# Sliding-window attention in quarter-array matmuls, with K, V and Q in natural order

## Chip, cores, metric

The kernel runs on one core of one Trainium2 chip. The metric is the device time of one launch in microseconds (us), lower is better. A run counts as slow when it is over 1.5% above the fastest of the same kernel; the ratios below use the other, fast runs alone.

## The reference

Eight samples, eight heads, 576 tokens, head size 64. Attention looks 32 tokens to each side; its result is the input of a two-layer MLP with 4608 tokens, 512 features and 2048 hidden units.

```python
scores = scale * np.matmul(q, k.transpose(0, 1, 3, 2))
mask = np.abs(pos[:, None] - pos[None, :]) <= 32
scores = np.where(mask, scores, -1e9)
attn = softmax(scores)                      # cut: written out with max, exp, sum
attn_out = np.matmul(attn, v)
x = attn_out.transpose(0, 2, 1, 3).reshape(B * S, H * D)
r = np.maximum(x @ w_in, 0.0)
out = (s * (r * r) + b) @ w_out             # float32 in and out
```

The kernel computes in bf16. The MLP is most of the work: for one sample of 576 tokens it takes 144 matmuls of 512 columns. At the 216 ns that one takes in the traces this is 31.1 us per sample.

## The kernel before: the parts that matter

The program first builds a list of tasks. Each has an engine (`pe`, `act`, `dve`, `pool`, `sp`), a list of instructions, an assumed cost in ns, what it reads and what it writes. A planner orders the tasks of every engine with those costs and sets the waits. On the chip each engine then runs its own list strictly in that order. Nearly all DMAs are issued by one engine, SP, so SP's list is a queue: an issue that is slow, or that waits, holds up every later one.

The samples from the third on (`b >= 2`) are prepared while the MLP of earlier samples runs. This is what SP does for 256 tokens of q or of k; rows of two tokens keep the pieces at 512 bytes, and one issue transposes all 256 tokens:

```python
def chunk(b, t0, n, key):                       # n = 128, 128, 32: 256, 256 and 64 tokens
    for name in "qk":
        add("sp", lambda e: e.dma_start(        # one load, 512-byte pieces
            STG[si][0:n, 0:1024].rearrange("p (h c) -> p h c", h=H),
            src_of[name][b, :, t0:t0 + 2 * n, :].rearrange("h (p i) d -> p h (i d)", i=2)),
            570.0, ...)
        add("dve", lambda e: e.tensor_copy(NAT[ni]..., STG[si]...), 680.0, ...)
        add("sp", lambda e: e.dma_start(        # one transposition of 128 x 1024
            dst[:, :, :, t0 // 2:t0 // 2 + n].rearrange("p i a s -> p (i a) s"),
            NAT[ni][0:n, :, :].rearrange("p i c -> p (i c)"), transpose=True),
            2500.0 * n / 128, ...)              # <- the assumed cost goes by size
    ...                                         # cut: DVE copies k into block diagonals KBD
```

v comes in 16 loads per sample issued by POOL. Attention on PE takes two heads at a time: K and V lie in block diagonals, so half of every 128 x 128 stationary matrix is zeros:

```python
fns = [lambda e: e.matmul(SC[:, par, pr * 128:pr * 128 + w],
       lhsT=KBD[:, pr, j, :], rhs=QT[slot][:, :, pr, lo // 2:hi // 2], ...) for pr in range(NPAIR)]
...                                             # cut: exp on ACT, mask on DVE
fns.append(lambda e: e.matmul(av[0:nr, pr, 0:130], lhsT=buf[:, pr, col:col + nr],
                              rhs=VBD[slot][:, j, pr, 0:130], ...))
...                                             # cut: XN = av / sum on DVE
add("sp", lambda e: e.dma_start(XT[:, :, ...], XN[xi][...], transpose=True), 1250.0, ...)   # b >= 3
```

The last line brings a result into the layout that the MLP reads. It too goes through SP's queue. For the first three samples (`XPE = 3`) PE does it. PE runs the visits of attention between the MLP's matmuls, as fillers of one list.

The softmax here doesn't subtract the row's maximum and nothing guards it: scores larger than these inputs give would overflow.

## Time and profile before

| | before |
|---|---|
| time, median of 3 runs | 330.35 us (329.95 to 333.12) |
| span of the profiled run | 329.0 us, mean granted clock 0.995 |
| PE busy | 307.3 us (93%) |
| MLP matmuls after 64 us, at their nominal spacing | 225.0 us |
| attention on PE after 64 us | 35.3 us |
| everything else on PE after 64 us (standing, slow clock) | 1.0 us |

The last three rows are worked out from the trace: each matmul is given the time from its start to the start of the next one, and an MLP matmul is charged 216 ns per 512 columns; what it takes beyond that is "everything else". In the kernels with quarters 93 ns per visit, the way into a visit (see below), are counted as attention. In the trace of before 31 of the 1344 records of MLP matmuls are missing, so its rows are good to about 1 us.

These lines are from the page of the kernel before. The row of 40 digits gives PE's busy tenths in 40 equal slices. The chain is the work that ended last, followed back from the end. In the group lines the columns are busy time, mean ns of one, and idle time of the engine before them with what ended it. In the lines of DMA issues they are KB each and us from issue to landing. The lines that begin with q are DMA queues: packets, MB, and the time that their packets took, as a share of the span of 16 DMA engines.

```profile
span 329.0 us, 5870 instructions
PE 307.3 (93%) x2212; PEld 179.6 (55%) x2245; DVE 207.8 (63%) x494; ACT 162.4 (49%) x275; POOL 87.4 (27%) x136
...
PE   1778989699999999999999999999999999999995
...
DMA packets 105372, 56.56 MB, mean 172 GB/s; under 512 B 54144, under 2 KB 97664, under 8 KB 105344
...
q1 hardware_dynamic: 100736, 49.10, 66.2%
q0 software_dynamic: 4608, 7.08, 10.5%
...
PE 71%; DMA 12%; SPq 8%; POOL 4%; issue 2%; DVE 1%; ACT 1%; ACTq 0%; DVEq 0%
...
L437 POOL DMA_DIRECT2D vst<-in_v_dram x96 | 59.0, 622 | 106.1 <-PE sc L548 60.5
...
L526 DVE COPY kbd<-kt 64x512 bf16<-64x512 bf16 (+1 forms) x72 | 18.6, 258 | 0.9
...
stg<-in_q_dram SPq DMA_DIRECT2D x16, 512.0 KB, 5.8
```

From the ninth slice on PE has nines alone, but for the last. The table of windows for 64 to 256 us says the same; its last line sums six stretches of 32 us:

```profile
sum 192.00, PE 190.32 PEld 106.67 DVE 142.47 ACT 100.15 POOL 54.45; mean PE 31.72 PEld 17.78 DVE 23.75 ACT 16.69 POOL 9.07
```

PE is the limit. The next lines are the views of SP's two lines in `chunk`, loads (L506) and transpositions (L519), with the time of one issue on SP as least/median/most in ns:

```profile
L506 SPq DMA_DIRECT2D stg<-in_q_dram x18: 333/396/2352, 55.3 to 224.8; - x18
L506 SPq DMA_DIRECT2D stg<-in_k_dram x18: 368/453/1953, 55.7 to 225.5; - x18
```

```profile
L519 SPq DMA_TRANSPOSE qt<-nat x18: 1174/1380/3882, 67.3 to 237.8; - x18
L519 SPq DMA_TRANSPOSE kt<-nat x18: 1192/1430/3731, 71.8 to 239.6; - x18
```

A transposition holds SP for 1.2 us at best and 1.4 us in the median. These medians mix two sizes. Told apart by the order of the issues, the 24 of 256 tokens, which the program books at 2500 ns, take 1.23 us at best and 2.07 us in the median (up to 3.88), and the 12 of 64 tokens, booked at 625 ns, take 1.17 and 1.26 us. So a quarter of the tokens is far from a quarter of the price.

### The profile page before, as it was taken

How to read it: one execution, taken by the hardware profiler on the slowest of the kernel's cores; microseconds unless marked ns; L12 is line 12 of the kernel's file. 1: busy time of each engine (PE TensorE's matmuls, PEld its weight loads, DVE VectorE, ACT ScalarE, POOL GpSimd, SP SyncE). 2: the span in 40 equal slices, each digit the busy share in tenths (PEclk: the TensorE clock that was granted, in tenths of full speed). 3: DMA queues.
4: the chain of work that ended last, by engine and by line, in shares of the span. 5: the costliest groups of instructions: out<-in, count | busy, mean ns of one | idle time of the engine just before them, and what ended most of it. 6: DMA issues, size and time to landing. Idle time of an engine off the chain costs nothing.

```text
span 329.0 us, 5870 instructions
## 1 busy us (share of the span) xinstructions
PE 307.3 (93%) x2212; PEld 179.6 (55%) x2245; DVE 207.8 (63%) x494; ACT 162.4 (49%) x275; POOL 87.4 (27%) x136
## 2 busy tenths in 40 slices
PE   1778989699999999999999999999999999999995
PEld 0567878576655565456545654555455544444442
DVE  6566577368867786869587857866876453323411
ACT  6686588146754672467236736541664433333300
POOL 8562341940560055014602440253000000000000
PEclk9999999799999999999999999999999999999999
DMA  8999999996599679968997998499913111000021
GB/s 212 227 368 356 299 179 266 290 203 156 136 238 212 159 160 216 194 179 229 203 253 125 230 224 194 133 201 244 225 36 75 51 46 62 34 32 34 32 85 76
DMA packets 105372, 56.56 MB, mean 172 GB/s; under 512 B 54144, under 2 KB 97664, under 8 KB 105344
## 3 DMA queue, kind: packets, MB, share of 16 engines
q1 hardware_dynamic: 100736, 49.10, 66.2%
q0 software_dynamic: 4608, 7.08, 10.5%
q8 instruction: 17, 0.28, 0.4%
q14 instruction: 11, 0.09, 0.1%
HBM read 36.70 MB, written 9.44 MB: 140 GB/s over the span
## 4 chain that ended last, share of the span: by engine, by line
PE 71%; DMA 12%; SPq 8%; POOL 4%; issue 2%; DVE 1%; ACT 1%; ACTq 0%; DVEq 0%
PE o L721 31%; PE w L702 30%; SPq L437 5%; DMA stg<-in_moe_w_out_dram 5%; PE avn L588 5%; DMA vst<-in_v_dram 4%; PE sc L548 3%; POOL vst L437 3%; DMA stg<-in_moe_w_in_dram 3%; SPq L461 2%; PE o L744 1%; POOL wout L420 1%; SPq L417 1%; DVE outs L734 0%; PE avn L610 0%
## 5 line engine op out<-in xcount | busy, mean ns | idle before, releaser
L702 PE MATMUL w<-xt,win 128*128 128x512 bf16 (+2 forms) x684 | 139.3, 340 | 1.3 <-ACT r L709 0.3
L721 PE MATMUL o<-wout,gt 128*128 128x512 bf16 (+1 forms) x629 | 139.8, 358 | 0.7 <-DVE outs L734 0.2
L709 ACT ACTIVATE r<-w 128x512 bf16<-128x512 f32 x144 | 85.9, 598 | 91.8 <-PE w L702 80.2
L711 DVE TENSOR_TENSOR gt<-r 128x512 bf16<-128x512 bf16 x144 | 60.9, 431 | 59.1 <-ACT r L709 58.1
L721 PEld LDWEIGHTS o<-wout,gt 128*128 128x128 bf16 x640 | 60.7, 98 | 57.6 <-DVE outs L734 0.7
L702 PEld LDWEIGHTS w<-xt,win 128*128 128x128 bf16 x704 | 62.0, 98 | 52.4 <-ACT r L709 0.8
L437 POOL DMA_DIRECT2D vst<-in_v_dram x96 | 59.0, 622 | 106.1 <-PE sc L548 60.5
L734 DVE SCALAR_TENSOR_TENSOR outs<-o,sb,cvec 128x512 f32<-128x512 f32 (+1 forms) x40 | 27.6, 692 | 19.1 <-PE o L721 17.5
L450 ACT CAST vbd<-vst 64x1024 bf16<-64x1024 f32 (+1 forms) x15 | 16.6, 1140 | 24.0 <-DMA vst<-in_v_dram 23.9
L565 ACT ACTIVATE exe<-sc 128x512 bf16<-128x512 f32 (+1 forms) x40 | 22.2, 554 | 10.8 <-PE sc L548 10.6
L588 PE MATMUL avn<-vbd,exo 128*128 128x130 bf16 (+1 forms) x224 | 26.1, 221 | 0.6 <-ACT xt L613 0.6
L548 PE MATMUL sc<-qt,kbd 128*128 128x128 bf16 (+1 forms) x288 | 25.2, 222 | 1.0 <-ACT exe L565 0.8
L548 PEld LDWEIGHTS sc<-qt,kbd 128*128 128x128 bf16 x288 | 20.2, 100 | 8.7 <-issue 1.0
L601 DVE TENSOR_TENSOR xn<-avn,rec 128x512 bf16<-128x512 f32 (+1 forms) x36 | 24.6, 683 | 0.3
L588 PE MATMUL avn<-vbd,exe 128*128 128x130 bf16 (+1 forms) x144 | 23.8, 221 | 0.5 <-ACT vbd L450 0.5
L511 DVE CAST nat<-stg 128x1024 bf16<-128x1024 f32 (+1 forms) x36 | 24.0, 682 | 0.1
L588 PEld LDWEIGHTS avn<-vbd,exo 128*128 128x128 bf16 (+1 forms) x224 | 20.8, 105 | 3.4 <-ACT xt L613 0.7
L565 ACT ACTIVATE exo<-sc 128x512 bf16<-128x512 f32 x32 | 19.2, 600 | 2.0 <-PE sc L548 2.0
L526 DVE COPY kbd<-kt 64x512 bf16<-64x512 bf16 (+1 forms) x72 | 18.6, 258 | 0.9
L588 PEld LDWEIGHTS avn<-vbd,exe 128*128 128x128 bf16 (+1 forms) x144 | 15.4, 110 | 3.2 <-ACT vbd L450 0.6
L598 DVE RECIPROCAL rec<-avn 128x8 f32<-128x8 f32 (+1 forms) x36 | 7.3, 204 | 13.7 <-PE avn L588 13.5
L571 DVE TENSOR_TENSOR exe<-exe,mask 128x512 bf16<-128x512 bf16 (+1 forms) x30 | 11.7, 389 | 4.8 <-ACT exe L565 4.7
(74 smaller groups left out, 152.1 us busy)
## 6 DMA issues: line engine op xcount, KB each, us to landing
stg<-in_q_dram SPq DMA_DIRECT2D x16, 512.0 KB, 5.8
stg<-in_k_dram SPq DMA_DIRECT2D x16, 512.0 KB, 7.4
out_dram<-outs SPq DMA_DIRECT2D x32, 256.0 KB, 2.3
vst<-in_v_dram POOLq DMA_DIRECT2D x96, 72.0 KB, 5.9
stg<-in_moe_w_in_dram SPq DMA_DIRECT2D x8, 512.0 KB, 8.5
stg<-in_moe_w_out_dram SPq DMA_DIRECT2D x8, 512.0 KB, 8.9
vst<-in_v_dram SPq DMA_DIRECT2D x16, 144.0 KB, 4.4
stg<-in_q_dram SPq DMA_DIRECT2D x8, 128.0 KB, 7.4
```

The lines of the kernel that those rows point to most:

```text
L437: add(stream, lambda e, dst=dst, src=src: e.dma_start(dst, src), 640.0 if stream == "sp" else 700.0, writes=[("VST", h, x) for x in (range ...
L511: add("dve", lambda e, si=si, ni=ni: e.tensor_copy(NAT[ni][0:n, :, :].rearrange("p i (h d) -> p h i d", h=H), STG[si][0:n, 0:1024].rearran ...
L526: add("dve", lambda e, i=i, p0=p0: e.tensor_copy(KBD[p0:p0 + 64, :, j0:j0 + nj, p0 + 32 * i:p0 + 32 * i + 32], KT[p0:p0 + 64, i, :, t0 // ...
L548: fns = [lambda e, j=j, pr=pr, lo=lo, hi=hi, w=w, par=par: e.matmul(SC[:, par, pr * 128:pr * 128 + w], lhsT=KBD[:, pr, j, :], rhs=QT[slot] ...
L565: add("act", lambda e, src=src, dst=dst: e.activation(dst.rearrange("p a (c i) -> p a c i", i=2), src, AF.Exp, bias=0.0, scale=0.125), 190 ...
L588: fns.append(lambda e, pr=pr, buf=buf, col=col, j=j, x=x, last=len(parts) - 1: e.matmul(av[0:nr, pr, 0:130], lhsT=buf[:, pr, col:col + nr] ...
L601: add("dve", lambda e: e.tensor_tensor(XN[xi][0:nr, :].rearrange("p (a b c) -> p a b c", a=4, b=2), av[0:nr, :, 0:128].rearrange("p a (b c ...
L702: add("pe", [lambda e, g=g, kc=kc: e.matmul(wt[:, g, :], lhsT=WIN_BF[:, kc, (f0 + g) * 128:(f0 + g + 1) * 128], rhs=XT[:, kc, t0 % XR:t0 % ...
L709: add("act", lambda e: e.activation(rt, wt, AF.Relu, bias=0.0, scale=1.0), 190 + 0.833 * 512, reads=[("W", wb)], writes=[("R1", rb)], key=key)
L711: add("dve", lambda e: e.tensor_tensor(GT[gs][:, f0:f0 + ng, g0:g0 + nt], rt, rt, ALU.mult), 130 + 0.53 * 512, reads=[("R1", rb)], writes= ...
L721: add("pe", [lambda e, fc=fc: e.matmul(O[:, ob, 0:cn], lhsT=GT[gs][:, fc, g0:g0 + 128], rhs=WOUT_BF[:, fc, c0:c0 + cn], start=(fc == 0), s ...
L734: add("dve", lambda e: e.scalar_tensor_tensor(OUTS[us][:, 0:cn], O[:, ob, 0:cn], SB128[:, 0:1], CVEC[:, c0:c0 + cn], ALU.mult, ALU.add), 2 ...
```

## The change

The intent: use TensorE as four independent quarters of 64 x 64. One head and 64 keys fit a quarter, so no block diagonals and no zeros are needed. Four scores, or four products with v, run at a time. The products with v of one unit (128 keys) and the scores of the next share one visit of PE. Without block diagonals, q, k and v can lie in natural token order, which saves the copies into the diagonals. The core of the diff:

```diff
-        KBD = sb((128, NPAIR, NTILE, 128), BF16, "kbd")
-        VBD = [sb((128, NTILE, NPAIR, VW), BF16, "vbd") for _ in range(2)]
+        KT = [sb((128, NPAIR, S), BF16, "kt") for _ in range(2)]
+        VB = [sb((128, NUNIT, H, VW), BF16, "vb") for _ in range(2)]
 ...
         def chunk(b, t0, n, key):
+            nx, np_ = (2, 128) if n == 256 else (1, n)
             for name in "qk":
-                add("sp", lambda e, si=si, name=name: e.dma_start(
-                    STG[si][0:n, 0:1024].rearrange("p (h c) -> p h c", h=H),
-                    src_of[name][b, :, t0:t0 + 2 * n, :].rearrange("h (p i) d -> p h (i d)", i=2)),
-                    570.0, ...)
+                add("sp", [lambda e, si=si, name=name, x=x: e.dma_start(
+                    STG[si][0:np_, x * 512:x * 512 + 512].rearrange("p (h d) -> p h d", h=H),
+                    src_of[name][b, :, t0 + 128 * x:t0 + 128 * x + np_, :].rearrange("h p d -> p h d"))
+                    for x in range(nx)],
+                    600.0 * nx, ...)
 ...
-                add("sp", lambda e, ni=ni, dst=dst: e.dma_start(
-                    dst[:, :, :, t0 // 2:t0 // 2 + n].rearrange("p i a s -> p (i a) s"),
-                    NAT[ni][0:n, :, :].rearrange("p i c -> p (i c)"), transpose=True),
-                    2500.0 * n / 128, ...)
+                add("sp", [lambda e, ni=ni, dst=dst, x=x: e.dma_start(
+                    dst[:, :, t0 + 128 * x:t0 + 128 * x + np_], NAT[ni][0:np_, x, :], transpose=True)
+                    for x in range(nx)],
+                    1250.0 * nx * np_ / 128, ...)
 ...
+        def load_v(b, t, key, waits=()):        # 5 loads a sample on SP, in place of 16 on POOL
+            add("sp", lambda e: e.dma_start(VST[0:n, t, :, :],
+                v[b, :, 128 * t:128 * t + n, :].rearrange("h p d -> p h d")), 640.0, ...)
 ...
+            fns = [lambda e, pr=pr, j=j, hp=hp: e.matmul(
+                SC[64 * (j % 2):64 * (j % 2) + 64, hp, pr * 128:pr * 128 + 128],
+                lhsT=KT[slot][64 * hp:64 * hp + 64, pr, 64 * j:64 * j + 64],
+                rhs=QT[slot][64 * hp:64 * hp + 64, pr, 64 * j:64 * j + 128], start=True, stop=True)
+                for pr in range(NPAIR) for j in tiles(u) for hp in hps]
 ...                                             # cut: products with v, joint visits, first two samples
-                cuts = [x0] + [x for x in range(XR, B * S, XR) if x0 < x < x0 + nr] + [x0 + nr]
+                cuts = {x0, x0 + r1 - r0} | {x for x in range(XR, B * S, XR) if x0 < x < x0 + r1 - r0}
+                cuts = sorted(cuts | ({x0 + WIN} if u == 0 else set()))   # one result transposition more a sample
```

The diff has three more parts: the loads of later samples may start earlier (`PACE`, the unit of the previous sample's attention that a load waits for, goes from 0 to 3 down to -1 to 1, where -1 is the last unit of the sample before that), NAT has 4 buffers in place of 6, and EX has 5 in place of 3.

## The prediction

> **What bounds the kernel now.** The span is 329.0 us (330.35 us by the clock). The chain that ended last is 71% PE; in the table of windows PE is busy 190.3 of 192.0 us between 64 and 256 us and 69.3 of 70.5 us after that. By matmul starts in the timeline, 64 to 326 us hold about 226 us of dense products (216 ns per 512-column matmul) and 34 us of attention, nothing idle. Before 64 us PE does only about 42 us of full-clock work (estimate: counts times 56 ns per 128 columns); there the chain is loads and casts of weights, the last w_out piece landing at 57.5 us; PE stands 2.8 us before the last column sum, then runs it at a reduced clock. DMA is 90 to 100% busy there, but moves 212 to 227 GB/s in the first 16 us (q, k, v) and 356 to 368 in the slices of weights.
>
> **Attention on PE, per sample from the third on:** 36 score matmuls at 56 ns (44 at the edges) and 52 value matmuls at 57: 4.86 us, 0.97 us a unit, 29 us for six samples.
>
> **What the change does.** Half of each of those matmuls multiplies zeros. Now 16 score matmuls (64x64, 128 columns) and up to 32 value matmuls (65 columns) per unit run four at a time: estimate 4 x 56 = 0.22 us and 8 x 29 = 0.24 us. The Trainium skill ("TensorEngine Tiling (Array Packing)", Key Properties) says that tiles work in parallel and that a change of tiling mode drains TensorE; no record of before shows such a change. A 128-column matmul lasts 220 ns at a spacing of 56: about 165 ns for a drain (estimate); one entering, one leaving and part of the wait between the value halves: about 0.33 us. Visit: 0.79 us instead of 0.97, 30 visits: minus 5.4 us, all on the saturated engine. The second sample saves about 1 us more.
>
> Against it: the first two samples' q and k are transposed in 144 blocks each in place of 48: about 2 us of PE more each; the first sample's visits are split, several us more, but PE idles there.
>
> **Moved off the other engines:** copies into block diagonals (18.6 us DVE), casts of v on ACT (16.6) and DVE (12), 96 loads issued by POOL (59 us). None was on PE's path after 64 us. Later q and k come in 256-byte pieces, v leaves the software queue: DMA roughly even, but SP issues about 20% more.
>
> **Start:** pairs of heads are loaded in 2304-byte pieces. At the weights' rate the 4.7 MB of q and k of two samples would take 13 us instead of 21. I count 3 to 5 us of earlier weights, shortening the hole at 57 to 64 us, less about 1.5 for the added PE work.
>
> **Sum:** 330.4 - 5.4 - 1 - 4 + 1.5, less about 2 for smoother supply = 319 us; range 312 to 326. Faster 0.75, same 0.23, slower 0.02.
>
> **To see:** a visit of about 0.8 us between dense matmuls; weights landed near 52 us; PE without idle after 60 us; dense products still at 216 ns.
>
> **What would make it wrong:** weight loads of 64 columns not running in parallel (a visit of 1.2 us or more, the gain gone); three full drains a visit; a longer first sample delaying the first dense matmul (23.8 us); SP issue or DMA falling behind from 60 to 240 us, so that PE starves.

## More of the kernel before

The timeline of SP shows how much room it has; its columns are start, us, what:

```profile
116.31 0.39 SPq L506 DMA_DIRECT2D stg<-in_q_dram  x1
117.36 1.28 SPq L618 DMA_TRANSPOSE xt<-xn  x1
120.25 0.40 SPq L506 DMA_DIRECT2D stg<-in_k_dram  x1
121.39 1.20 SPq L618 DMA_TRANSPOSE xt<-xn  x1
123.05 0.37 SPq L506 DMA_DIRECT2D stg<-in_q_dram  x1
124.19 2.48 SPq L618 DMA_TRANSPOSE xt<-xn  x2
```

There are gaps of 0.5 to 1.6 us between issues. Summed over 80 to 280 us, SP's issues take 125.5 of 200 us.

## The result

The changed kernel takes 369.52 us (median of 4 runs, 368.26 to 371.17); the kernel before, on the same chip, 330.56 us. The ratio is 1.1163, with a 95% interval of 1.1099 to 1.1227: slower. A ratio here and below is the mean time of one kernel's fast runs over that of the other's of the same rounds, so it is not quite the ratio of the medians.

| | before | after |
|---|---|---|
| span of the profiled run | 329.0 us | 369.4 us |
| mean granted clock | 0.995 | 0.949 |
| MLP matmuls after 64 us, at nominal spacing | 225.0 us | 226.9 us |
| attention on PE after 64 us | 35.3 us | 27.7 us |
| everything else on PE after 64 us | 1.0 us | 46.8 us |

So the attention saved 7.6 us of PE, as hoped, and PE lost 45.8 us by standing and by a slower clock. (The 12 gaps on PE of over 0.4 us after 64 us sum to 32 us; the rest, about 15 us, is mostly the slower clock.) With the 1.9 us of the first row the sum is 40.1 of the 40.4 us between the spans. Everything lies after 64 us. The profiled run is the slowest of the four and the one with the lowest clock; the others had 0.961 to 0.977.

The same lines of the page, after:

```profile
span 369.4 us, 8204 instructions
PE 319.2 (86%) x3452; PEld 169.3 (46%) x3452; DVE 176.7 (48%) x376; ACT 141.7 (38%) x217; POOL 42.6 (12%) x64
...
PE   3679997979699569674999997979699999999996
...
PEclk9999999899889889995999998998989999999999
...
DMA packets 150661, 56.71 MB, mean 154 GB/s; under 512 B 137312, under 2 KB 142432, under 8 KB 150624
...
q1 hardware_dynamic: 150624, 56.19, 66.1%
...
PE 54%; DMA 18%; SPq 17%; DVE 6%; issue 3%; ACT 1%; POOL 0%; DVEq 0%
...
stg<-in_q_dram SPq DMA_DIRECT2D x24, 256.0 KB, 4.2
```

PE's row has holes from the seventh slice to the 29th (about 55 to 268 us), roughly as long as SP prepares attention; then it is full again. All other engines became less busy, as intended. The share of SP's queue in the chain that ended last doubled from 8 to 17%. The DMA engines did not get more to do: the packets of the two queues before took 76.7% of 329.0 us, 252 us, and those of the one queue after 66.1% of 369.4 us, 244 us, although there are 43% more of them. The windows of 64 to 256 us, summed:

```profile
sum 192.00, PE 162.68 PEld 79.07 DVE 92.72 ACT 74.78 POOL 17.50; mean PE 27.11 PEld 13.18 DVE 15.45 ACT 12.46 POOL 2.92
```

PE is 27.6 us less busy there than before. That is not because a visit is dear. The timeline of PE, around one joint visit:

```profile
91.33 0.81 PE L711 MATMUL w<-xt,win 128*128 128x512 bf16 x3
92.07 0.32 PE L550 MATMUL avn<-vb,ex 64*64 64x65 bf16 x16
92.22 0.39 PE L498 MATMUL sc<-qt,kt 64*64 64x128 bf16 x16
92.47 0.32 PE L550 MATMUL avn<-vb,ex 64*64 64x65 bf16 x16
92.72 0.83 PE L730 MATMUL o<-wout,gt 128*128 128x256 bf16 x5
```

The 48 quarter matmuls take 0.65 us from 92.07 to 92.72 us. In the single records the quarters of a group of four start 2 to 5 ns apart. Before the first quarter the last MLP matmul holds PE for 309 instead of 216 ns, and the last quarter is followed by the next MLP matmul only after 122 ns. A change of mode thus costs about 93 ns on the way in, in every visit that did not stall, and about as much on the way out. All told a visit takes 0.74 us, where a unit took 0.97.

What did get dearer is the supply. SP's two lines in `chunk`, after (loads L463, transpositions L475):

```profile
L463 SPq DMA_DIRECT2D stg<-in_q_dram x30: 432/723/3344, 46.7 to 259.5; - x30
L463 SPq DMA_DIRECT2D stg<-in_k_dram x30: 596/887/2711, 51.3 to 260.2; - x30
```

```profile
L475 SPq DMA_TRANSPOSE qt<-nat x30: 1173/1267/2258, 68.3 to 272.3; - x30
L475 SPq DMA_TRANSPOSE kt<-nat x30: 1224/1267/2762, 71.0 to 274.9; - x30
```

A transposition of 128 tokens takes SP 1.27 us in the median, about as long as one of 256 tokens at its best before (1.23, median 2.07), and there are 60 in place of 36. A load with 256-byte pieces takes 0.7 to 0.9 us in place of 0.4 to 0.45, and there are also 60 in place of 36. And v's loads came to SP. Summed over the whole traces, the transpositions of q and k went from 69.6 to 81.9 us of SP, but the loads of q and k from 24.2 to 57.9 us: the loads grew most. Between 80 and 280 us SP's issues now take 191.0 of 200 us.

How that reaches PE is seen in the chain that ended last, in order of time (start, us, what). Line L421 is a load of v, L588 the transposition of a result that the MLP and the next result's buffer wait for:

```profile
120.39 0.88 PE w L711 x4
121.27 0.90 SPq L421
...
122.21 1.27 SPq L421
...
123.53 1.14 SPq L463
...
127.09 2.00 SPq L463
...
129.13 1.88 SPq L588
...
131.05 2.36 DMA xt<-xn
...
133.44 0.70 DVE xn L572
...
134.19 0.32 PE avn L550 x16
...
134.90 2.73 PE w L711 x8
```

From 121.3 to 129.1 us SP issues loads of the next sample, one after the other. Only then comes the transposition of a result, L588, which was planned behind them. Its landing frees a buffer, for which DVE waits with the next result, and for that PE waits in turn: it stands for 3.15 us before 134.19. Then the clock is down (the record has half the clock from 135.7 us for 3.4 us): eight MLP matmuls take 2.73 us, where eight times 216 ns are 1.73. Of this same kind are 23.3 us of waits of DVE (last line); the waits of all engines show that loads come late too. The columns are total us, times, longest:

```profile
ACT ex L519 <- PE avn L550: 39.5, 21, 7.3
DVE nat L470 <- DMA stg<-in_q_dram: 29.9, 9, 6.2
DVE xn L572 <- DMA xt<-xn: 23.3, 10, 5.3
```

### The profile page after: what moved, and what is told of

Read it like the earlier page. It is cut to its first block, busy times and chain, and to the rows that moved or that the text cites. A ratio compares the mean times of both kernels' runs of the same rounds, so it can differ in the third digit from the quotient of the medians.

```text
span 369.4 us, 8204 instructions
## 1 busy us (share of the span) xinstructions
PE 319.2 (86%) x3452; PEld 169.3 (46%) x3452; DVE 176.7 (48%) x376; ACT 141.7 (38%) x217; POOL 42.6 (12%) x64
## 2 busy tenths in 40 slices
DMA packets 150661, 56.71 MB, mean 154 GB/s; under 512 B 137312, under 2 KB 142432, under 8 KB 150624
## 3 DMA queue, kind: packets, MB, share of 16 engines
q1 hardware_dynamic: 150624, 56.19, 66.1%
## 4 chain that ended last, share of the span: by engine, by line
PE 54%; DMA 18%; SPq 17%; DVE 6%; issue 3%; ACT 1%; POOL 0%; DVEq 0%
PE o L730 25%; PE w L711 23%; SPq L463 6%; DMA xt<-xn 4%; DMA stg<-in_moe_w_out_dram 3%; DMA stg<-in_q_dram 3%; PE avn L550 3%; SPq L421 3%; SPq L588 2%; SPq L475 2%; DMA out_dram<-outs 2%; DMA vst<-in_v_dram 2%; DMA qt<-nat 2%; PE sc L498 2%; DVE ex L523 1%
## 5 line engine op out<-in xcount | busy, mean ns | idle before, releaser
L711 PE MATMUL w<-xt,win 128*128 128x512 bf16 (+2 forms) x704 | 152.4, 354 | 1.4 <-DMA xt<-xn 1.4
L730 PE MATMUL o<-wout,gt 128*128 128x512 bf16 (+1 forms) x640 | 151.7, 371 | 1.6 <-DVE outs L743 1.4
L519 ACT ACTIVATE ex<-sc 128x1024 bf16<-128x1024 f32 (+3 forms) x45 | 41.3, 927 | 43.9 <-PE avn L550 39.5
L550 PE MATMUL avn<-vb,ex 64*64 64x65 bf16 x1024 | 24.6, 205 | 30.4 <-DVE ex L523 13.4
L428 POOL CAST vb<-vst 128x512 bf16<-128x512 f32 (+1 forms) x37 | 25.2, 681 | 199.4 <-DMA vst<-in_v_dram 199.1
L550 PEld LDWEIGHTS avn<-vb,ex 64*64 64x64 bf16 x1024 | 16.5, 114 | 46.3 <-DVE ex L523 17.1
L743 DVE SCALAR_TENSOR_TENSOR outs<-o,sb,cvec 128x512 f32<-128x512 f32 (+1 forms) x40 | 27.7, 692 | 20.3 <-PE o L730 12.0
L572 DVE TENSOR_TENSOR xn<-avn,rec 128x512 bf16<-128x512 f32 (+1 forms) x36 | 24.8, 688 | 23.9 <-DMA xt<-xn 23.3
L523 DVE TENSOR_TENSOR ex<-ex,mask 128x1024 bf16<-128x1024 bf16 (+3 forms) x45 | 28.7, 644 | 3.9 <-ACT ex L519 3.5
L498 PE MATMUL sc<-qt,kt 64*64 64x128 bf16 x576 | 20.8, 238 | 2.3 <-DVE kt L454 1.1
L498 PEld LDWEIGHTS sc<-qt,kt 64*64 64x64 bf16 x576 | 13.9, 118 | 3.9 <-ACT ex L519 1.6
L410 POOL CAST wout<-stg 128x1024 bf16<-128x1024 f32 x6 | 6.4, 1062 | 8.9 <-DMA stg<-in_moe_w_out_dram 8.9
```

The lines of the kernel that those rows point to most:

```text
L428: (lambda e: e.tensor_copy(VB[slot][0:n, t, :, 0:D], VST[0:n, t, :, :])),
L498: fns = [lambda e, pr=pr, j=j, hp=hp: e.matmul(SC[64 * (j % 2):64 * (j % 2) + 64, hp, pr * 128:pr * 128 + 128], lhsT=KT[slot][64 * hp:64 * ...
L519: add("act", lambda e, dst=dst, src=src: e.activation(dst, src, AF.Exp, bias=0.0, scale=0.125), 190 + 0.833 * 512 * len(hs), reads=[("SC", ...
L523: add("dve", lambda e, flat=flat, mask=mask: e.tensor_tensor(flat, flat, mask, ALU.mult), 130 + 0.53 * 512 * len(hs), reads=[("E", ei, hp) ...
L550: return [lambda e: e.matmul(av[64 * x:64 * x + 64, h, 0:D + 1], lhsT=buf[64 * g:64 * g + 64, h % 2, h // 2, c:c + 64], rhs=VB[slot][64 * ...
L572: add("dve", lambda e: e.tensor_tensor(XN[xi][0:p1, :].rearrange("p (a c) -> p a c", a=H), av[0:p1, :, 0:D], REC[ri][0:p1, :].rearrange("p ...
```

## The experiments

The theories, as the expectations below call them:

- S: SP's in-order queue is overloaded. A DMA issue costs SP time by its kind, not by its bytes, and the change raised the number of issues. What arrives late makes DVE, ACT and PE wait in turn.
- D: the DMA engines are at fault. 256-byte pieces are inefficient, and with more packets everything lands later.
- C: joint visits are at fault: products with v of one unit and scores of the next must both be ready, so a delay of either holds both.
- B: there are too few buffers (NAT was cut from 6 to 4, XN stays at 2).

All results in one table. "SP" is the sum of SP's issues between 80 and 280 us of the profiled run, of 200. Every group of runs shares its runs of the kernel before; those had medians between 330.95 and 332.49 us.

| run | median us | ratio to before [95%] | SP, us of 200 |
|---|---|---|---|
| before | 330.56 | 1 | 125.5 |
| after | 369.52 | 1.1163 [1.1099, 1.1227] | 191.0 |
| v_pool | 360.82 | 1.0885 [1.0827, 1.0944] | 189.3 |
| qk_act | 351.17 | 1.0613 [1.0570, 1.0657] | 144.2 |
| big_pieces | 361.04 | 1.0902 [1.0831, 1.0974] | 190.3 |
| split_visits | 371.97 | 1.1222 [1.1162, 1.1283] | 187.5 |
| x_pe | 349.25 | 1.0508 [1.0421, 1.0595] | 156.7 |
| x_pe_qk_act | 358.44 | 1.0792 [1.0686, 1.0897] | 105.0 |
| x_pe_v_pool_qk_act | 356.67 | 1.0704 [1.0607, 1.0800] | 82.2 |
| x_pe_v_pool | 349.08 | 1.0528 [1.0456, 1.0601] | 150.6 |
| before_v_sp | 343.59 | 1.0345 [1.0257, 1.0432] | 151.4 |
| before_sp_issues | 364.12 | 1.0980 [1.0889, 1.1071] | 177.4 |
| before_tr2 | 351.34 | 1.0593 [1.0493, 1.0693] | 159.3 |
| few_issues | 335.25 | 1.0096 [1.0026, 1.0167] | 156.7 |
| few_issues_x_pe | 335.12 | 1.0096 [1.0025, 1.0168] | 114.6 |
| after_buf | 366.22 | 1.1051 [1.0970, 1.1131] | 190.5 |
| few_buf | 331.30 | 1.0018 [0.9925, 1.0111] | 157.2 |
| few_x_pe_buf | 334.45 | 1.0086 [0.9999, 1.0172] | 113.1 |
| few_k_pool | 339.62 | 1.0148 [1.0071, 1.0224] | 135.0 |
| few_big_k | 325.16 | 0.9779 [0.9735, 0.9823] | 146.5 |

Two of these kernels, big_pieces and few_big_k, give a wrong result. The comparison with the reference passed all the same: q and k are drawn at a tenth of unit variance, so all weights inside the window are nearly equal, and a score at the wrong key changes little. With q scaled by 30 and k by 10 the valid ones stay at a relative error of 0.007, these two are at 1.2 and more.

### First group: which part of the change

**v_pool**: v's five loads go back to POOL.

```diff
-            add("sp", lambda e: e.dma_start(VST[0:n, t, :, :], ...), ..., dma=("l", n // 2, 18.0))
+            add("sp" if b < 2 else "pool", lambda e: e.dma_start(VST[0:n, t, :, :], ...), ..., dma=("l" if b < 2 else "v", ...))
```

> The changed kernel, but the loads of v from the third sample on are issued by POOL (software queue) instead of SP: about 30 issues fewer on SP, bytes and pieces of DMA unchanged. Theory S (the SP queue, busy 191 of 200 us between 80 and 280 us, hands PE its data too late): PE's idle time falls by at least the 19 us of issue taken away, 345 to 353 us. Theory D (the 16 DMA engines, loaded with 256-byte pieces, are the limit): within 2% of 369.5 us. Theory C (the joint visit couples late data of one unit to its neighbour): within 2% of 369.5.

Measured: 360.82 us, 8.7 less than after. Less came back than S had expected. SP was no freer: 189.3 of 200 us, since the loads of k took longer to issue (37.6 us in place of 24.2 in the same window). Freed time on SP was filled up by other issues that got slower. The test is not clean between S and D: on the software queue v's bytes go in packets of 4096 bytes, and the packets fell from 150661 to 124741, so the pieces did not stay as they were.

**qk_act**: q's and k's loads are issued by ACT.

```diff
-                add("sp", [lambda e, si=si, name=name, x=x: e.dma_start(
+                add("act", [lambda e, si=si, name=name, x=x: e.dma_start(
```

> The changed kernel, but the loads of q and k from the third sample on are issued by the ACT queue, 60 issues fewer on SP (45 us of SP's 191 us in the window from 80 to 280 us); same bytes and pieces. Theory S: most of the lost 39 us comes back, 332 to 345 us. Theory D: within 2% of 369.5 us. Theory C: within 2% of 369.5.

Measured: 351.17 us, and SP is down to 144.2. Nearly half of the loss comes back, with the same pieces and the same bytes on the DMA engines, though through a second hardware queue (q10 in its page). That speaks for S, though S alone had expected more.

**big_pieces**: the same number of issues, but q and k in 512-byte pieces (two tokens a row, so the result is wrong).

```diff
-                    STG[si][0:np_, x * 512:x * 512 + 512].rearrange("p (h d) -> p h d", h=H),
-                    src_of[name][b, :, t0 + 128 * x:t0 + 128 * x + np_, :].rearrange("h p d -> p h d"))
+                    STG[si][np_ // 2 * x:np_ // 2 * x + np_ // 2, 0:1024].rearrange("p (h c) -> p h c", h=H),
+                    src_of[name][b, :, t0 + 128 * x:t0 + 128 * x + np_, :].rearrange("h (p i) d -> p h (i d)", i=2))
```

> Wrong result on purpose: the changed kernel with q and k of the third sample on loaded as pieces of 512 bytes into half the partitions per issue: the same number of issues and bytes, half as many pieces for q and k. Theory D: DMA load falls, the time falls by 10 us or more (below 359 us). Theory S in its plain form (a cost per issue): within 2% of 369.5; in a second form (SP's time per issue goes with the number of pieces): 355 to 365 us.

Measured: 361.04 us. Packets fell from 150661 to 123013 and 8.5 us came back. So pieces do matter, but they are about a fifth of the loss. By which way is open. The time of the packets on the DMA engines did not fall (70.7% of 360.9 us, 255, against 244), which speaks against D. The q and k loads took SP 37.5 us in place of 45 between 80 and 280 us, but SP's sum stayed at 190.3.

**split_visits**: the two products in visits of their own.

```diff
-            t = pe_part(due(...), av_part(*last[0]) if last else None, qk_part(b, u))
-            exp_mask(b, u)
-            close(t)
+            close()
+            pe_part(due(b, u), sc=qk_part(b, u))
+            exp_mask(b, u)
```

> The changed kernel with the value product of a unit and the score product of the next in two visits of PE instead of one, nothing else. Theory C: a unit is finished without waiting for the next unit's q and k, the time falls by 10 us or more (below 359 us). Theory S and D: within 2% of 369.5 us, or slower by up to 8 us for 34 more changes of tiling mode and unhidden half waits.

Measured: 371.97 us, no faster than after. C falls, in the form tested.

### Second group: relieve SP further, and load the old kernel

**x_pe**: the results of all samples are transposed by PE, not through SP's queue.

```diff
-XPE = 3
+XPE = 8
```

> The changed kernel with the transposes of the attention's result done on PE for all samples, not only the first three: about 30 DMA transposes of 1.25 us or more of SP each go away (38 us of SP's 191 in the window from 80 to 280 us), PE gets 4 matmuls of 56 ns per unit more (about 6 us in all). Theory S: the time falls by 15 us or more, 338 to 354 us. Theory D (DMA bytes and pieces): those transposes are 4.7 MB of 56.7, so a fall of at most 3% minus 6 us of PE: 362 to 372 us.

Measured: 349.25 us (6 runs); SP at 156.7. Half of the loss comes back (the bytes fell from 56.71 to 53.77 MB, less than the 4.7 MB that I had expected), although PE now has 5 samples' transpositions more to do.

**x_pe_qk_act** and **x_pe_v_pool_qk_act**: the edits above together.

> Both: results transposed on PE, and q and k loads of the third sample on issued by ACT. SP is left with the v loads, the transposes of q and k and the stores, about 21 us a sample where PE needs 35. Theory S: PE no longer stands after 80 us, 318 to 332 us. Theory D: no better than the run with the q and k loads on ACT alone (351 us) by more than 3%, 340 to 352 us.

> All three: results transposed on PE, q and k loads on ACT, v loads on POOL from the third sample on. Theory S: SP has less to do than in the kernel before; 316 to 330 us, not slower than the run without the v loads on POOL by more than 1%. Theory D: 340 to 352 us.

Measured: 358.44 and 356.67 us. Both missed by far: SP is relieved to 105 and 82 us of 200, yet the kernels are slower than x_pe alone. The waits of ACT in x_pe_qk_act suggest why:

```profile
ACT r L721 <- issue: 12.7, 2, 6.5
ACT ex L519 <- issue: 11.9, 3, 6.2
ACT xt L584 <- issue: 11.8, 2, 7.4
```

ACT stood up to 7.4 us while none of its instructions waited for data; in this longest gap 6.1 us were DMA issues. On ACT, relu and exp queue behind an issue. That this is the cause is not shown: qk_act has gaps of the same kind on ACT (eight of 5.5 to 7.1 us) and gained all the same.

**before_v_sp**: the kernel before, with its 96 small loads of v issued by SP.

```diff
-                    load_v(b, h, due(b, 0) - 30.0 + 0.1 * h, "pool", ...)
+                    load_v(b, h, due(b, 0) - 30.0 + 0.1 * h, "sp", ...)
```

> The kernel before, with its 96 loads of v from the third sample on issued by SP instead of POOL, nothing else: 96 issues of at least 0.64 us each, 61 us more of SP in the 176 us in which it had 129 us to do. Theory S: the old kernel loses PE time in the same way, 340 to 365 us. Theory D (same bytes and pieces): within 2% of 330.6 us.

Measured: 343.59 us, with SP at 151.4 of 200. This is a first sign in the old kernel that issues on SP cost time. It also moves v from the software to the hardware queue, which raised the packets from 105372 to 129946, so it is not a clean test.

### Third group: the decisive pair

**before_sp_issues**: the kernel before, with the same bytes, the same 512-byte pieces, the same copies and the same assumed costs, so the same planned order. Each load of q and k is cut by partitions into four issues (two for the last 64 tokens), and each transposition into two.

```diff
-                add("sp", lambda e, si=si, name=name: e.dma_start(
-                    STG[si][0:n, 0:1024]..., src_of[name][b, :, t0:t0 + 2 * n, :]...),
+                cut = n // (4 if n == 128 else 2)
+                add("sp", [lambda e, si=si, name=name, r=r: e.dma_start(
+                    STG[si][r:r + cut, 0:1024]..., src_of[name][b, :, t0 + 2 * r:t0 + 2 * r + 2 * cut, :]...)
+                    for r in range(0, n, cut)],
                     570.0, ...
-                add("sp", lambda e, ni=ni, dst=dst: e.dma_start(
-                    dst[:, :, :, ...].rearrange("p i a s -> p (i a) s"), NAT[ni][0:n, :, :]..., transpose=True),
+                add("sp", [lambda e, ni=ni, dst=dst, i=i: e.dma_start(
+                    dst[:, i, :, t0 // 2:t0 // 2 + n], NAT[ni][0:n, i, :], transpose=True) for i in (0, 1)],
                     2500.0 * n / 128, ...
```

> The kernel before with nothing changed but the number of issues on SP from the third sample on: each load of q or k in four issues (two for the short one) by partitions, each DMA transpose in two; same bytes, same 512-byte pieces, same planned order. About 14 loads of 0.35 us and 6 transposes of 1.25 us more a sample, SP's least work goes from about 18 to 30 us a sample, which is what the changed kernel has. Theory S: PE starves in the old kernel too, 340 to 362 us. Theory D (DMA bytes and pieces): within 2% of 331 us.

Measured: 364.12 us, 32.2 more than the kernel before in the same rounds. None of the new attention is in it. From its page, and from the view of its line of transpositions:

```profile
PE 317.2 (88%) x2245; PEld 181.5 (50%) x2245; DVE 208.7 (58%) x494; ACT 162.4 (45%) x275; POOL 87.3 (24%) x136
...
PE   2778998988999599949989699979895999999996
```

```profile
L521 SPq DMA_TRANSPOSE qt<-nat x36: 1188/1264/2338, 66.6 to 270.6; - x36
L521 SPq DMA_TRANSPOSE kt<-nat x36: 1177/1250/2827, 71.7 to 273.2; - x36
```

PE's row has holes of the same kind as after the change. Half a transposition takes 1.25 us in the median, where a whole one took 2.07 (256 tokens) or 1.26 (64): two halves are dearer than a whole, and SP's time for these transpositions went from 69.6 to 99.1 us. SP is at 177.4 of 200 us. This shows that more issues, with no smaller pieces of data, make the old kernel about as slow as the new one. (Each further issue also adds small packets: 107869 in all, against 105372.) The plan was kept, with prices that were now wrong; whether a plan with the measured prices would lose less was not tested, here or for the changed kernel.

**few_issues**: the other direction. The changed kernel keeps its quarters, but q comes in rows of two again (one load, one transposition per 256 tokens), k keeps natural order but is transposed in one issue per 256 tokens (its tile is laid out as blocks of 128 keys), and v is issued by POOL. Of the eight issues for q and k of 256 tokens, five are left.

```diff
+        QT2 = [... .rearrange("p (i a s) -> p i a s", i=2, a=NPAIR) for x in QT]
+        KTB = [sb((128, NUNIT, NPAIR, 128), BF16, "kt") for _ in range(2)]
 ...
-                    dst[:, :, t0 + 128 * x:t0 + 128 * x + np_], NAT[ni][0:np_, x, :], transpose=True)
-                    for x in range(nx)], ...
+                    dst = KTB[slot][:, t0 // 128:t0 // 128 + nx, :, 0:np_].rearrange("p x a s -> p (x a) s")
+                    src = NAT[ni][0:np_, 0:nx, :].rearrange("p x c -> p (x c)")
+                add("sp", lambda e, dst=dst, src=src: e.dma_start(dst, src, transpose=True), 1300.0, ...)
```

> The changed kernel with fewer and larger issues from the third sample on: q in rows of two (512-byte pieces, one load and one transpose per 256 queries), k natural with one transpose per 256 keys (its tile laid out by blocks of 128 keys), v issued by POOL. SP has per sample 8 loads, 6 transposes, the result's 6.4 transposes and 4.5 stores, about 21 us at least; PE's work is that of the changed kernel. Theory S: PE hardly stands, 316 to 330 us. Theory D: the pieces of k and v stay at 256 bytes, so about half of the way, 340 to 355 us.

> The same with the result's transposes on PE for all samples: SP's least work falls to about 13 us a sample, PE gets about 6 us more in all. Theory S: no starving left, but PE does more: 318 to 330 us, within 2% of the run without it. Theory D: 340 to 355 us.

Measured: 335.25 us and, with PE transposing all results, 335.12 us. The first gives back 34 of the 39 us lost, with the quarters, the joint visits and the natural order of k and v all in place. But few_issues is not a test of the issues alone: q has its 512-byte pieces again, v is on the software queue, and the packets fell from 150661 to 109957. It also shows that SP's sum does not set the loss: it is 156.7 as in x_pe, which takes 14 us more. The second run shows that a further relief of SP, to 114.6, gives nothing in total: by the accounting of the last table PE's "everything else" falls by 5 us and attention with its transpositions grows by 4.

**x_pe_v_pool**: x_pe and v_pool together.

> The changed kernel with the result's transposes on PE and the v loads on POOL, nothing on ACT: SP's least work about 20 us a sample, DMA pieces all at 256 bytes. Theory S: 325 to 340 us (better than the 349 of the result's transposes alone, and without the run that put loads on ACT and made ACT wait for the queue). Theory D: 342 to 352 us.

Measured: 349.08 us, no better than x_pe alone. A miss for S, as I had put it: the gain of v_pool and that of x_pe do not add. SP was hardly freer, at 150.6 against 156.7.

### Fourth group: threshold, buffers

**before_tr2**: only the second half of before_sp_issues, the transpositions in two.

> The kernel before with only its DMA transposes of q and k split in two (6 issues of 1.25 us more a sample, SP's least work 18 to 25.5 us a sample; it was busy 73% of the time). Theory S as a threshold (PE needs 35 us a sample): a small loss, 331 to 342 us, far less than half of the 32 us that both splits cost. If the loss goes in proportion to the issues' time: about 60% of it, 345 to 353 us.

Measured: 351.34 us, 20.2 more than the kernel before, about 60% of what both halves of that edit cost. SP is at 159.3. So a threshold at full load falls: here PE stands with a queue that is 80% busy. Nor does the share decide alone, since few_buf below loses nothing at 157.2. I take it that what counts is whether an urgent issue is stuck behind others; no run changes that order alone.

**after_buf**, **few_buf**, **few_x_pe_buf**: more buffers, in the changed kernel and in the two with fewer issues (few_x_pe_buf has XN at 3).

```diff
-        NSTG, NNAT, NEX, NXN, NR1, NOUT, XR = 9, 4, 5, 2, 3, 3, 2048
+        NSTG, NNAT, NEX, NXN, NR1, NOUT, XR = 9, 6, 5, 4, 3, 5, 2048
```

> The changed kernel with more buffers only (XN 4 for 2, NAT 6 for 4, OUTS 5 for 3), the same issues. Theory S: SP stays the limit, within 3% of 369.5 us. Theory B (buffers: engines stand on a buffer that a late DMA frees): 345 to 358 us.

> The version with fewer issues on SP, with the same more buffers. The waits that it still has (DVE for a transpose of XN to land, 10 us; for a store to land, 3 us; for a late q) go: 318 to 328 us, faster than the kernel before. If B plays no part: 333 to 337 us.

> Fewer issues, the result's transposes on PE, more buffers (XN 3, NAT 6, OUTS 5). PE does about 6 us more than in the version beside it but SP has nothing urgent left: 322 to 331 us. If B plays no part: 333 to 337 us.

Measured: 366.22 us, 331.30 us and 334.45 us. In the changed kernel the buffers are worth 3 us, so B falls as the cause. few_buf equals the kernel before (ratio 1.0018); I had expected it to be faster.

### Last two: what keeps the repaired version from winning

**few_k_pool**: few_buf, with k's loads issued by POOL as well.

```diff
-                    add("sp", [lambda e, si=si, x=x: e.dma_start(
+                    add("pool", [lambda e, si=si, x=x: e.dma_start(
```

> The version with fewer issues and more buffers, with the loads of k from the third sample on issued by POOL too. SP's work in the window from 80 to 280 us falls from 157 to about 126 us, the level of the kernel before (129 of 176). Theory S: the standing after 64 us falls from 16 us to below 6 us and the saving of PE shows: 317 to 326 us, faster than the kernel before by 2% or more. If the standing has another cause (POOL late with its casts of v behind its own waits, order of the in-order DVE): 328 to 336 us.

Measured: 339.62 us (6 runs, three of them slow). The three fast ones took 334.15 to 338.15 us, and their ratio, 1.0148, has an interval that overlaps that of few_buf, so it is not faster, and whether it is slower is unclear. Its profile fell in a slow execution, so I build nothing on it beyond its SP sum of 135.0. Why less work on SP did not help is not settled.

**few_big_k**: few_buf, with k in 512-byte rows of two, one load per 256 keys (wrong result: the keys are then not in natural order).

```diff
-                    add("sp", [lambda e, si=si, x=x: e.dma_start(
-                        STG[si][0:np_, x * 512:x * 512 + 512]..., k[b, :, t0 + 128 * x:t0 + 128 * x + np_, :]...) for x in range(nx)],
+                    add("sp", lambda e, si=si: e.dma_start(
+                        STG[si][0:n, 0:1024]..., k[b, :, t0:t0 + 2 * n, :].rearrange("h (p i) d -> p h (i d)", i=2)),
```

> Wrong result on purpose: the version with fewer issues and more buffers, with k loaded like q, two rows to a piece (512 bytes) and one issue per 256 keys, so that the keys come in the wrong order. If what remains comes from the loads of k in natural order (their pieces and second issue; 31 us of SP in the window of 200 us): 318 to 326 us and standing after 64 us below 8 us. If it is another cause: 328 to 335 us.

Measured: 325.16 us (6 runs, 324.31 to 326.72), ratio 0.9779 [0.9735, 0.9823], so 2.2% faster, with an interval that reaches across the 2% line. It is the only kernel faster than the one before, and it is not correct. It says what the natural order of k costs in the repaired version: 2.4% by the two ratios, give or take about 1%. I found no correct form of it. With k in rows of two, the 64 stationary columns would have to be read as two runs of 32, and the builder accepts a stationary operand with one free dimension only; that kernel did not build.

PE's time after 64 us, by the same accounting as above:

| us | MLP at nominal spacing | attention | everything else |
|---|---|---|---|
| before | 225.0 | 35.3 | 1.0 |
| after | 226.9 | 27.7 | 46.8 |
| before_sp_issues | 226.5 | 42.3 | 23.3 |
| few_buf | 225.8 | 25.9 | 13.5 |
| few_big_k (wrong result) | 225.8 | 25.5 | 5.2 |

The profile of few_buf is of its slowest run, 335.33 us, so its last figure is on the high side. In before_sp_issues a part of the standing lies inside the visits and is counted as attention. The saving by quarters, 8 to 10 us, is there in each kernel that has them. What differs is how much of it the supply eats.

## Why the prediction was wrong

It was wrong in the direction: 319.0 us predicted, 369.52 measured.

**Right: the cost of a visit.** Predicted 0.79 us in place of 0.97, measured 0.74 (0.65 and 0.093 for the way in). I took the parallel quarters and the drain at a change of mode from the Trainium skill ("TensorEngine Tiling (Array Packing)", Key Properties). The trace agrees with both: the matmuls of a group of four start 2 to 5 ns apart, and each change costs about 93 ns. (The prediction says that no record of before shows a change. At 48.44 us one probably does: a 256-column matmul before transpositions of 32 rows holds PE 205 ns in place of 108.) My estimate had the drains too dear (0.33 us; measured about 0.19 for both) and the matmuls too cheap (0.46 us; 0.56 remain of 0.74). The formula in "TensorE: Matmul & The Clock Gate" (Part 3, Measured speedup vs the span model), which adds about 4 ns for each further tile of a group, would have been nearer: with 56 ns from the trace of before and 29 as half of its 57, 4 x 68 + 8 x 41 gives an estimate of 0.60 us.

**Right: PE gains.** Attention fell by 7.6 us after 64 us, for 5.4 and about 1 predicted.

**Wrong by sign: "about 2 for smoother supply", and the 4 us of an earlier start.** The last cast of weights did move forward, from 59.2 to 54.5 us. But the MLP work done by 64 us is 25.5 us against 26.0, so nothing came of it.

**The step that failed: "DMA roughly even, but SP issues about 20% more".** I named SP falling behind as a risk and gave it no time in the sum. The 20% are what the program's own constants say. Per sample they add up to 6 x 570 + 2 x (2500 + 2500 + 625) + 5.4 x 1250 + 4.5 x 600 ns = 24 us of SP before, and to 10 x 600 + the same 11.25 us + 5 x 640 + 6.0 us of results + 2.7 us of stores = 29 us after. In these sums the split of the transpositions costs nothing, because they are booked by size, and a load costs what it did. The traces say otherwise: in that of before 64 tokens take 1.26 us in the median, where 625 ns were booked, and after the change a load of q or k takes 0.97 us in the mean, where 600 ns were booked. With means over each whole trace (v: from the third sample on) a sample takes SP:

| per sample, us | before | after |
|---|---|---|
| q, k loads | 6 x 0.67 = 4.0 | 10 x 0.97 = 9.7 |
| q, k transpositions | 6 x 1.93 = 11.6 | 10 x 1.36 = 13.6 |
| v loads | 0 (POOL) | 5 x 0.86 = 4.3 |
| result transpositions | 5.4 x 1.34 = 7.2 | 6.4 x 1.46 = 9.4 |
| stores | 4.5 x 0.49 = 2.2 | 4.5 x 0.61 = 2.7 |
| sum | 25.0 | 39.7 |

PE needs 31.1 us for the MLP of a sample and 3.7 for five visits, 34.8 together. So the change raised SP's work by nearly 60%, not 20%, to more than PE takes, in a queue that runs in a fixed order; in the window of 200 us SP's sum rose by 52%. The largest part of the rise, 5.7 of 14.7 us, are the loads of q and k, then v's loads with 4.3. And where the sum had a gain of 2 us for smoother supply, PE stood and ran slowly for 45.8 us more. It could have been seen beforehand: with durations from the trace of before alone, 16.4 transpositions of q, k and results at 1.25, 15 loads at 0.4 and the stores at 2 us give an estimate of 28 to 29 us a sample, against a little under 19 by the same count for the kernel before.

**What the experiments show, and what they only suggest.** That more issues on SP can cause a loss of this size is shown by before_sp_issues. That fewer issues together with some larger pieces give nearly all of it back is shown by few_issues. That the pieces of 256 bytes have a share is shown by big_pieces (8.5 us); few_big_k points the same way, but it also has fewer issues. The Trainium skill ("DMA: Bandwidth & Descriptors", Specifications) says that line rate needs 512 bytes or more; in the trace of before a 256-byte packet takes 26 ns in the mean and a 512-byte packet 35 ns, which agrees: half the bytes in three quarters of the time. (The comparison is loose: four fifths of these 256-byte packets are of transpositions.) S in its plain form, a price by kind alone, does not hold: 1.26 against 2.07 us for 64 and 256 tokens. That the DMA engines were simply overloaded is not what the traces show: their packets took 244 us after and 252 before. How the causes divide is open, because fewer and larger pieces also change the issue. Two rivals stand untested. No run gave the planner the measured prices or put the result's transposition ahead of the loads, so the loss may come from the wrong order as much as from the load. And no run took the earlier `PACE` of the loads back; it is not the cause alone, since few_issues keeps it and before_sp_issues lacks it. Open too is why the relief of SP by v_pool, qk_act and x_pe gives less than the sum on SP suggests: the issues left behind got longer (up to 3.6 us for a load of k in v_pool), which looks like back-pressure from the DMA engines, but no run here separates it.

**Why the loss is larger than the lateness.** With or just after seven of the twelve stalls after 64 us the record of the clock shows half the clock for 3.4 us or a multiple of it (2.73 us for work of 1.73 in the case above), and the mean granted clock is 0.949. There PE pays for a wait twice.

## What to carry to other kernels

Count the issues on the queue that issues the DMAs, price each with its duration in the trace by kind and size, and compare the sum per round with what the bounding engine needs per round; a planner's cost constants are not a measurement, and a price by bytes can mislead. When a compute change forces a new data layout, cost the layout's loads and transpositions first: here it took six times what the quarters gained (45.8 us of PE against 7.6). Moving issues to another engine is no sure relief: qk_act alone gained 18 us, and added to x_pe it made the kernel 9 us slower.

## What the Trainium skill lacked or had wrong

- "DMA: Bandwidth & Descriptors" gives no time that a DMA transposition holds the issuing sequencer on trn2; it has only cycle counts of "previous generations" in its part on trn3. Here it is 1.16 to 1.23 us at best on SP, for 64, 128 and 256 tokens of 512 values alike, but 2.07 us in the median for 256 tokens in the kernel before; plain loads of q and k take 0.33 to 0.6 us at best.
- The same page (Issuing engines are not separate DMA queues) says that issuing from several engines only saves the time to initiate, "which is usually small relative to the DMA itself". Here it was not small: a transposition holds SP 1.27 us and lands 2.5 us after its issue, and before_sp_issues lost 32.2 us by more issues of the same bytes.
- I found no page that says how long issues made by ACT hold up its compute: in x_pe_qk_act ACT stood up to 7.4 us, 6.1 of them in issues.
- "TensorEngine Tiling (Array Packing)" (Key Properties) says that a change of mode drains TensorE, without a size: here about 93 ns each way between 128 x 128 and 64 x 64.
